# One more probability buffer, fewer copied scores, a regrouped load order and a five-block last unit in a fused attention and feed-forward kernel

## Chip, cores and metric

The kernel runs on one core of one Trainium2 chip. The metric is device time in microseconds for one execution. Before the change the median of three runs is 1485.19 us (1485.15 to 1485.42).

## What is computed

With x of 2048 tokens by 512 features, 32 heads of 16 and a hidden width of 1792:

```python
xn = layernorm(x)
q, k, v = split(xn @ wqkv)                       # 32 heads of 16
s = softmax(q @ k.T * 16 ** -0.5) @ v            # per head, all 2048 keys
s = concat_heads(s) @ wo
g = silu(ffn), ffn = (silu(xn @ w_gate) * (xn @ w_up)) @ w_down
out = x + s * g
```

All is float32. Most products are split in a high and a low part and take three matrix products.

## The kernel before, in words

**Three stages.** A prologue (0 to about 160 us) normalises x, projects q, k and v for four blocks of 512 tokens and writes them to DRAM (q_d, k_d, v_d, with row shifts for the exponentials in sh_d). Then comes the attention, with the feed-forward layer and the output projection woven into it as filler. A tail projects the last 512 tokens. The prologue's tile pools are closed before the attention's pools open, so the attention's tiles lie where prologue tiles lay, and their first writers wait for the last users of these, the store of v_d (L812 issues it) among them.

**Units and blocks.** A unit is one group of 4 heads (g) with one block of 512 queries (b): 8 x 4 = 32 units. A unit runs over 16 key tiles of 128 keys, cut into blocks of 4 to 6 key tiles (L448 to L462; units 27, 29, 30 and 31 have four blocks of 4, unit 28 has 6, 6, 4, the others 5s and one 6). There are 100 blocks, numbered from 0.

**Inside a block** (`run`, L837). For n key tiles there are 2n pairs (key tile, j), each with the scores of two heads. TensorE makes the two score products of a pair side by side on two halves of the array (L853). A pair goes one of two ways:
- *direct* ("D"): both products go to one of two double PSUM buffers (score0, score1); ScalarE takes the exponential of 128 x 1024 values straight into a probability buffer (L869), which frees the PSUM buffer.
- *copied* ("A", then "B"): the first head's product goes to a spare PSUM bank (acc1), VectorE copies it to a probability buffer (L881), then the second head's product goes to the same bank and is copied (L887). ScalarE takes the exponential in place later, after all direct ones of the block (L893).

Between them stands filler ("F"): pairs of half-array products (L188) of the feed-forward layer or of the output projection, in chunks that end in VectorE work on the banks bankx and banky. Feed-forward chunks have 24 products (gate and up, ended by the tanh of L219 on ScalarE and L220, L221 on VectorE) or 21 (down, ended by L238 and L239 or L242 and L243); chunks of the output projection have 9 or 12 (ended by L351 and L352). A block takes the length of the next chunk as its amount of filler. When all scores of a block are out, `values` (L373) multiplies the probabilities of its key tiles with v, four heads side by side into acc0 (L377). The program order on TensorE is thus: scores and filler of a block, its values, the next block.

**Who sets the order.** `events(n, f)` (L464) places D, A, B and F on a line of product slots by hand; the number of copied pairs comes from n and f. A block is written below as (n, f, copied), for example (6, 21, 3). VectorE's other work (splits of weights into high and low parts, normalising a finished unit) is a list of chores with costs, put between copies where the plan has room (L889), and the rest at the block's end. Each engine takes its instructions in program order. SP issues nearly all loads in program order, too: keys (`load_k`, six issues), values (`load_v`, one), queries (`load_q`, six), shifts (`load_shift`, two), gate and up weights (`load_gu`, two, L127) and down weights (`load_wd`, one, L150, into a single buffer). Keys and values have a ring of five chunks (kst, vst), queries two (qst).

**Buffers.** The probability buffers ("pr", 4 KB a partition each) are a ring of PROBS = 11, taken pair by pair in program order and freed when the values have read them. A block of 6 key tiles takes 12.

**Tail.** After the last block the rest of the filler runs (L916), then the last unit is normalised in two halves (L951 to L956: transpose, reciprocal, product, transpose), projected with wo (L932), gated and stored.

Of the kernel before, what the change touches and what calls it, by code (L numbers as in the profile page):

```python
# [9 lines left out]
F32 = mybir.dt.float32  # L10
# [9 lines left out]
P = 128  # L20
# [3 lines left out]
DH = 16  # L24
F = 1792
NB = 4
TB = S // NB
# [12 lines left out]
DC = D // HALF  # L40
LIMIT = 160.0
EARLY = 2
PROBS = 11
EPS = 1e-5
FINE = (27, 29, 30, 31)
QSLOT = (0, 1, 0)
# [4 lines left out]
def tile_block(ctx: ExitStack, tc: tile.TileContext, x, wqkv, wo, w_gate, w_up, w_down, out):  # L51
# [16 lines left out]
    two = ctx.enter_context(tc.tile_pool(name="two", bufs=2))  # L68
    pone = ctx.enter_context(tc.tile_pool(name="pone", bufs=1, space=PSUM))

    ident = const.tile([P, P], F32, name="ident")
    make_identity(nc, ident)
    bankx = pone.tile([P, 512], F32, name="bankx")
    banky = pone.tile([P, 512], F32, name="banky")
    banks = (bankx, banky)
# [40 lines left out]
    def load_v(g, c):  # L116
        sp.dma_start(vst[(g * NB + c) % RING], v_d[g][:, c * CT:(c + 1) * CT])
# [262 lines left out]
    def normalise(u, first, last, between=None):  # L380
        g, b = divmod(u, NB)
        n = last - first
        o1 = late.tile([P, TB], F32, tag="o1", name="o1")
        rl = late.tile([P, TB // 32], F32, tag="rl", name="rl")[:, :n // 32]
        ov = o1[:, :n].rearrange("p (c d) -> p c d", d=32)
        dst = on[b][:, first:last].rearrange("p (c s d) -> p c s d", s=2, d=DH)[:, :, g % 2]
        yield 3, partial(dve.transpose, o1[:, :n], acc[0][:, first:last])
        yield 1, partial(dve.reciprocal, rl, ov[:, :, DH])
        if between:
            yield 3, between  # L390
        yield 2, partial(dve.tensor_mul, dst, ov[:, :, :DH], rl[:, :, None].to_broadcast([P, n // 32, DH]))

    def finish(u):
        g, b = divmod(u, NB)
        chores.extend(normalise(u, 0, TB))
        if g % 2:
            o2 = late.tile([P, TB], F32, tag="o2", name="o2")

            def turn_out():
                dve.transpose(o2, on[b])  # L400
                if g < NG - 1 or b == NB - 1:
                    pool.dma_start(o_d[g // 2, b], o2)

            chores.append((3, turn_out))
            if g == NG - 1 and b < NB - 1:
                whole = (hh, wd, hh)[b].rearrange("p f j t -> p (f j) t")
                lhs[b, DT - 1] = whole[:, 2 * (DT - 1)], whole[:, 2 * DT - 1]

                def rounded():
                    dve.tensor_copy(lhs[b, DT - 1][0], o2)  # L410
                    ready[b] += 1

                chores.append((2, rounded))
                chores.append((3, lambda: dve.tensor_sub(lhs[b, DT - 1][1], o2, lhs[b, DT - 1][0].bitcast(F32))))

    settled = mybir.DependencyInfo(mybir.DependencyClass.Sync, mybir.DependencyReason.DATA)
    units = NG * NB
# [30 lines left out]
    blocks, opened = [], []  # L448
    for u in range(units):
        opened.append(len(blocks))  # L450
        if u in FINE:
            ns = [4] * 4
        elif u == units - 4:
            ns = [6, 6, 4]
        else:
            ns = [5] * 3
            far = sizes[len(blocks):len(blocks) + 3]
            ns[far.index(max(far)) if far[1] < max(far) else 1] = 6
        kt = 0
        for n in ns:  # L460
            blocks.append((u, kt, n))
            kt += n  # L462

    def events(n, f):  # L464
        length = 2 * n + f
        copied = max(0, 2 * n - max(2, (10 * length + 46) // 40)) if f else 0
        direct = 2 * n - copied
        gap = max(4, min(5, (length - 8) / max(1, direct - 2)))
        marks = [(0, "D"), (1, "D")] + [(7 + gap * i, "D") for i in range(direct - 2)]
        marks += [(4 + (length - 6) * i / (2 * copied), "AB"[i % 2]) for i in range(2 * copied)]  # L470
        marks.sort()
        out = []
        at = left = 0
        for t, kind in marks:
            while left < f - 1 and at < t:
                out.append((at, "F"))
                left += 1
                at += 1
            out.append((at, kind))
            at += 1 if kind == "D" else 0.5  # L480
        return direct, out + [(at + i, "F") for i in range(f - left)]

    with ExitStack() as pro:
# [4 lines left out]
        plast = pro.enter_context(tc.tile_pool(name="plast", bufs=1))  # L488
        pps = pro.enter_context(tc.tile_pool(name="pps", bufs=4, space=PSUM))

        xin = facc

        def load_tile(t):
# [85 lines left out]
        def turn(t):  # L579
            for c in range(DT):  # L580
                nc.tensor.transpose(acc[t % 2][:, c * P:(c + 1) * P], xn[t][:, c * P:(c + 1) * P], ident)  # L581
            return acc[t % 2].rearrange("p (c f) -> p c f", f=P)
# [239 lines left out]
    spare_bank = acc[1]  # L822
    ring(2, RING, att)
    queries(1, att)
    for c in range(2, NB):
        load_k(0, c)
        load_v(0, c)
    gate = [w.rearrange("p f j t -> p (f j) t")[:, 12 + i].bitcast(F32) for w in (hh, wd) for i in range(2)]
    on = [att.tile([P, TB], F32, name=f"on{b}") for b in range(NB)]

# [6 lines left out]
    def run(u, first, n):  # L837
        nonlocal lower
        g, b = divmod(u, NB)
        q = qst[u % 2]  # L840
        f = 0 if blocked() or not sizes else sizes.pop(0)
        direct, todo = events(n, f)
        if now == 0:
            for _ in range(4):
                todo.insert(0, todo.pop(max(i for i, (_, e) in enumerate(todo) if e == "F")))
        pairs = [(kt, j) for kt in range(first, first + n) for j in range(2)]
        straight, copies = pairs[:direct], pairs[direct:]
        probs, waiting = {}, []

        def scores(bank, kt, j, h):  # L850
            k, kc = kst[(g * NB + kt // CT) % RING], kt % CT
            r = slice(h * HALF, h * HALF + NROW)
            mm(bank, k[r, j, kc * P:(kc + 1) * P], q[r, j], start=True, stop=True)  # L853

        done = 0
        copying = [t + 1.5 for t, e in todo if e in "AB"]
        final = len(todo) - 1
        free = 0
        for at, (t, e) in enumerate(todo):
            if at == final:  # L860
                tidy()
            if e == "F":
                fill(1)
            elif e == "D":
                kt, j = straight[done]
                for h in order():
                    scores(score[done % 2][:, h], kt, j, h)
                probs[kt, j] = ppool.tile([P, 2, TB], F32, tag="pr", name="pr")
                act(probs[kt, j], score[done % 2], AF.Exp, scale=0.25)  # L869
                done += 1  # L870
                if done == 2:
                    while ends:
                        ends.pop(0)()
                    out_steps()
            elif e == "A":
                kt, j = copies.pop(0)
                waiting.append((kt, j))
                scores(spare_bank, kt, j, 0)
                lower = True
                probs[kt, j] = ppool.tile([P, 2, TB], F32, tag="pr", name="pr")  # L880
                dve.tensor_copy(probs[kt, j][:, 0], spare_bank)  # L881
                free = copying.pop(0) + 3
            else:
                kt, j = waiting[-1]
                scores(spare_bank, kt, j, 1)
                lower = False
                dve.tensor_copy(probs[kt, j][:, 1], spare_bank)  # L887
                free = copying.pop(0) + 3
            while chores and at < final and (not copying or max(free, t) + chores[0][0] <= copying[0] + 0.5):  # L889
                free = max(free, t) + chores[0][0]  # L890
                chores.pop(0)[1]()
        for kt, j in waiting:
            act(probs[kt, j], probs[kt, j], AF.Exp, scale=0.25)  # L893
        tidy()
        out_splits()
        catch_up()
        values(u, range(first, first + n), probs)

    for now, (u, first, n) in enumerate(blocks):
        g, b = divmod(u, NB)  # L900
        if first == 0 and u + 1 < units:
            load_q(u + 1)
            load_shift(u + 1)
        if first == 0 and g + 1 < NG and b == 0:
            load_k(g + 1, 0)
            load_v(g + 1, 0)
        run(u, first, n)
        if b == NB - 1 and g + 1 < NG:
            for c in range(NB - 1):
                if first < (c + 1) * CT <= first + n:  # L910
                    load_k(g + 1, c + 1)
                    load_v(g + 1, c + 1)
        if first + n == KT and u + 1 < units:
            ends.append(partial(finish, u))
# [80 lines left out]
```

## Time and profile before

| | |
|---|---|
| median of three runs | 1485.19 us |
| the profiled execution | 1483.91 us |
| its span, first to last instruction | 1482.1 us |
| mean granted TensorE clock | 0.989 |
| TensorE busy | 1448.6 us |
| ScalarE busy | 1091.7 us |
| VectorE busy | 765.3 us |
| GpSimd busy | 89.8 us |

The profile counts an engine busy while an instruction's record lasts. TensorE overlaps matmuls, so its share says little about waits between them. Rows in time give start, length, engine, line of the kernel, tiles written and read, and in brackets the idle time ahead with what ended it. PE is TensorE, PEld its weight loads, ACT ScalarE, DVE VectorE, POOL GpSimd, SPq the queue of loads. PEclk is the clock that TensorE was granted, as a share of the full one.

### The profile page before, as it was taken

To read this page: it belongs to the slowest core of one execution; us is meant where nothing else is said; L and a number is where in the kernel's file an instruction comes from. 1 tells how busy PE (TensorE), PEld (TensorE's weight loads), DVE (VectorE), ACT (ScalarE), POOL (GpSimd) and SP (SyncE) were. 2 spreads that over 40 slices of the span, in tenths; PEclk is the share of its full clock that TensorE was granted. 3 is DMA by queue.
4 is the path that set the end of the run, shared out by engine and by line. 5 is a ranking of instruction groups with operands and counts; after the bars stand their busy time and mean duration, and the time that the engine had idled before them with its cause. 6 is when DMAs were issued, how large, how long until landed. Compare 5 with 4: busy or idle time off the path is not lost.

```text
span 1482.1 us, 27795 instructions
## 1 busy us (share of the span) xinstructions
PE 1448.6 (98%) x11227; PEld 873.7 (59%) x11227; DVE 765.3 (52%) x1295; ACT 1091.7 (74%) x1235; POOL 89.8 (6%) x104
## 2 busy tenths in 40 slices
PE   9999799999999999999999999999999999999998
PEld 7777565566555665655566556665555665544444
DVE  5543255355545554555456435555554464455646
ACT  6733467787788888777887778888778787766674
POOL 4100200000000000000000000000000000001232
PEclk9999999999999999999999999999999999999999
DMA  6778632034544511345324202482342221323231
GB/s 222 262 242 255 145 76 55 12 84 94 115 101 104 127 33 34 71 117 124 92 74 117 53 18 70 105 172 62 83 102 58 55 69 55 90 72 118 83 114 66
DMA packets 126956, 148.17 MB, mean 100 GB/s; under 512 B 12524, under 2 KB 79340, under 8 KB 126052
## 3 DMA queue, kind: packets, MB, share of 16 engines
q1 hardware_dynamic: 121620, 125.79, 33.7%
q0 software_dynamic: 4912, 20.12, 3.7%
q8 instruction: 91, 1.49, 0.4%
q14 instruction: 45, 0.37, 0.1%
q10 hardware_dynamic: 288, 0.39, 0.1%
HBM read 106.68 MB, written 39.58 MB: 99 GB/s over the span
## 4 chain that ended last, share of the span: by engine, by line
PE 93%; DVE 3%; ACT 1%; DMA 1%; SPq 1%; issue 0%; DVEq 0%; ACTq 0%
PE acc L377 30%; PE bankx L188 23%; PE score L853 15%; PE banky L188 10%; PE ps L606 6%; PE acc L853 5%; PE ps L608 3%; DVE pr L881 1%; DMA wdr<-in_B_w_down_dram 1%; SPq L100 1%; DVE pr L887 1%; ACT pr L869 0%; PE acc L581 0%; ACT pr L893 0%; DMA v_d<-vt 0%
## 5 line engine op out<-in xcount | busy, mean ns | idle before, releaser
L869 ACT ACTIVATE pr<-score 128x1024 f32<-128x1024 f32 x854 | 813.6, 1028 | 293.2 <-PE score L853 258.9
L377 PE MATMUL acc<-pr,vst 128*17 128x512 f32 x4096 | 478.8, 596 | 0.0
L853 PE MATMUL score<-qst,kst 50*128 50x512 f32 x1708 | 420.5, 419 | 0.1
L188 PE MATMUL bankx<-fx,guh 64*128 64x512 f32 x896 | 313.4, 396 | 6.5 <-DVE ga L220 6.4
L188 PE MATMUL banky<-fx,guh 64*128 64x512 f32 x896 | 312.8, 396 | 0.4 <-DVE ga L221 0.3
L377 PEld LDWEIGHTS acc<-pr,vst 128*17 128x17 f32 x4096 | 114.6, 97 | 309.6 <-issue 269.4
L853 PEld LDWEIGHTS score<-qst,kst 50*128 50x128 f32 x1708 | 187.7, 186 | 137.1 <-issue 74.0
L881 DVE COPY pr<-acc 128x512 f32<-128x512 f32 x170 | 117.5, 691 | 189.4 <-PE acc L853 188.7
L188 PE MATMUL bankx<-wd,hh 64*128 64x512 f32 x672 | 205.6, 394 | 0.0
L188 PE MATMUL banky<-wd,hh 64*128 64x512 f32 x672 | 195.8, 394 | 0.0
L188 PEld LDWEIGHTS bankx<-fx,guh 64*128 64x128 f32 x896 | 167.9, 188 | 22.9 <-DVE ga L220 7.0
L188 PE MATMUL bankx<-fx,gul 64*128 64x512 f32 x448 | 177.4, 396 | 0.0
L188 PE MATMUL banky<-fx,gul 64*128 64x512 f32 x448 | 176.7, 394 | 0.0
L887 DVE COPY pr<-acc 128x512 f32<-128x512 f32 x170 | 117.6, 692 | 109.7 <-PE acc L853 99.6
L893 ACT ACTIVATE pr<-pr 128x1024 f32<-128x1024 f32 x170 | 172.8, 1064 | 0.0
L188 PEld LDWEIGHTS banky<-fx,guh 64*128 64x128 f32 x896 | 167.6, 188 | 5.9 <-DVE ga L221 1.9
L853 PE MATMUL acc<-qst,kst 50*128 50x512 f32 x340 | 144.8, 426 | 17.9 <-DVE pr L881 12.8
L188 PEld LDWEIGHTS bankx<-wd,hh 64*128 64x128 f32 x672 | 124.8, 187 | 13.8
L188 PEld LDWEIGHTS banky<-wd,hh 64*128 64x128 f32 x672 | 124.5, 186 | 5.0
L220 DVE SCALAR_TENSOR_TENSOR ga<-th,bankx 128x512 f32<-128x512 f32 x56 | 38.5, 687 | 154.7 <-ACT th L219 154.7
L853 PEld LDWEIGHTS acc<-qst,kst 50*128 50x128 f32 x340 | 63.7, 187 | 54.7 <-DVE pr L881 26.9
L188 PEld LDWEIGHTS bankx<-fx,gul 64*128 64x128 f32 x448 | 84.6, 189 | 6.7
(174 smaller groups left out, 1341.0 us busy)
## 6 DMA issues: line engine op xcount, KB each, us to landing
gur<-in_B_w_gate_dram SPq DMA_DIRECT2D x56, 256.0 KB
gur<-in_B_w_up_dram SPq DMA_DIRECT2D x56, 256.0 KB
wdr<-in_B_w_down_dram SPq DMA_DIRECT2D x56, 256.0 KB
kst<-k_d SPq DMA_DIRECT2D x192, 64.0 KB
qst<-q_d SPq DMA_DIRECT2D x192, 64.0 KB
fx<-xt_d SPq DMA_DIRECT2D x24, 512.0 KB
q_d<-parts SPq DMA_DIRECT2D x16, 512.0 KB
k_d<-parts SPq DMA_DIRECT2D x16, 512.0 KB
```

The lines of the kernel that those rows point to most:

```text
L100: sp.dma_start(dst[r:r + DH].bitcast(F32), src[part].rearrange("(j h d) t -> h d j t", j=2, h=2)[h])
L188: mm(banks[i], lhs[halves[i]], rhs[halves[i]], start=start, stop=stop)
L220: dve.scalar_tensor_tensor(ga, th, 1.0, bankx, op0=ALU.add, op1=ALU.mult)
L377: mm(acc[0][h * 32:h * 32 + DH + 1], v[:, kt % CT, h * (DH + 1):(h + 1) * (DH + 1)], probs[kt, h // 2][:, h % 2], start=kt == 0, stop=kt = ...
L606: mm(ps, w, a[:, c], start=n == 0, stop=n == 3 * DT - 1)
L608: mm(ps, a[:, c, tokens], w, start=n == 0, stop=n == 3 * DT - 1)
L853: mm(bank, k[r, j, kc * P:(kc + 1) * P], q[r, j], start=True, stop=True)
L869: act(probs[kt, j], score[done % 2], AF.Exp, scale=0.25)
L881: dve.tensor_copy(probs[kt, j][:, 0], spare_bank)
L887: dve.tensor_copy(probs[kt, j][:, 1], spare_bank)
L893: act(probs[kt, j], probs[kt, j], AF.Exp, scale=0.25)
```

## The change

- PROBS goes from 11 to 12. The room comes from two places: the identity matrix moves into a pool of the prologue, and the two 2 KB transpose buffers of `normalise` and `finish` ("o1", "o2") become one ("o"), taken when the work runs.
- `events` caps the copied pairs at (2 length - 5) // 22, where length is the number of scores and filler products, starts the copied products at slot 3 and puts them at least 5.6 slots apart. Block 0 gets no copied pair. Of the plan's blocks, (6, 21, 3) becomes (6, 21, 2), (4, 12, 2) and (4, 9, 3) become (4, 12, 1) and (4, 9, 1), and block 0 goes from one copied pair to none; (6, 24, 2), (5, 24, 1) and (5, 21, 2) keep their counts. In all, 148 pairs are copied, which were 170.
- The last unit is cut 4, 3, 3, 3, 3, so there are 101 blocks, as many as chunks of filler.
- Loads ahead of unit 0: the keys and values of chunk 3 are issued after block 0, the queries and shifts of unit 1 after block 1, the first keys and values of group 1 ahead of block 2. They all stood ahead of block 0's loads.

```diff
-PROBS = 11
+PROBS = 12
...
-    ident = const.tile([P, P], F32, name="ident")
-    make_identity(nc, ident)
...
     def normalise(u, first, last, between=None):
         g, b = divmod(u, NB)
         n = last - first
-        o1 = late.tile([P, TB], F32, tag="o1", name="o1")
-        rl = late.tile([P, TB // 32], F32, tag="rl", name="rl")[:, :n // 32]
-        ov = o1[:, :n].rearrange("p (c d) -> p c d", d=32)
+        turned = {}
...
+        def turn():
+            turned[0] = late.tile([P, TB], F32, tag="o", name="o")[:, :n]
+            dve.transpose(turned[0], acc[0][:, first:last])
...
     def finish(u):
...
-            o2 = late.tile([P, TB], F32, tag="o2", name="o2")
+            o = {}
 
             def turn_out():
-                dve.transpose(o2, on[b])
+                o[0] = late.tile([P, TB], F32, tag="o", name="o")
+                dve.transpose(o[0], on[b])
...
-        if u in FINE:
+        if u == units - 1:
+            ns = [4, 3, 3, 3, 3]
+        elif u in FINE:
             ns = [4] * 4
...
     def events(n, f):
         length = 2 * n + f
-        copied = max(0, 2 * n - max(2, (10 * length + 46) // 40)) if f else 0
+        need = 2 * n - max(2, (10 * length + 46) // 40)
+        copied = max(0, min(need, (2 * length - 5) // 22)) if now else 0
         direct = 2 * n - copied
         gap = max(4, min(5, (length - 8) / max(1, direct - 2)))
         marks = [(0, "D"), (1, "D")] + [(7 + gap * i, "D") for i in range(direct - 2)]
-        marks += [(4 + (length - 6) * i / (2 * copied), "AB"[i % 2]) for i in range(2 * copied)]
+        marks += [(3 + max(5.6, (length - 5) / (2 * copied)) * i, "AB"[i % 2]) for i in range(2 * copied)]
...
+        ident = pc.tile([P, P], F32, name="ident")
+        make_identity(nc, ident)
...
-    for c in range(2, NB):
-        load_k(0, c)
-        load_v(0, c)
+    load_k(0, 2)
+    load_v(0, 2)
...
     for now, (u, first, n) in enumerate(blocks):
         g, b = divmod(u, NB)
-        if first == 0 and u + 1 < units:
+        if first == 0 and 0 < u < units - 1:
             load_q(u + 1)
             load_shift(u + 1)
-        if first == 0 and g + 1 < NG and b == 0:
+        if now == 2 or first == 0 and 0 < g < NG - 1 and b == 0:
             load_k(g + 1, 0)
             load_v(g + 1, 0)
         run(u, first, n)
+        if now == 0:
+            load_k(0, NB - 1)
+            load_v(0, NB - 1)
+        elif now == 1:
+            load_q(1)
+            load_shift(1)
```

More of the change, by code (lines that the diff above doesn't have):

```diff
@@ L382, in normalise, with invert, scaled @@
         n = last - first
-        o1 = late.tile([P, TB], F32, tag="o1", name="o1")
-        rl = late.tile([P, TB // 32], F32, tag="rl", name="rl")[:, :n // 32]
-        ov = o1[:, :n].rearrange("p (c d) -> p c d", d=32)
+        turned = {}
         dst = on[b][:, first:last].rearrange("p (c s d) -> p c s d", s=2, d=DH)[:, :, g % 2]
-        yield 3, partial(dve.transpose, o1[:, :n], acc[0][:, first:last])
-        yield 1, partial(dve.reciprocal, rl, ov[:, :, DH])
+        def turn():
+            turned[0] = late.tile([P, TB], F32, tag="o", name="o")[:, :n]
+            dve.transpose(turned[0], acc[0][:, first:last])
+        def invert():
+            ov = turned[0].rearrange("p (c d) -> p c d", d=32)
+            turned[1] = late.tile([P, TB // 32], F32, tag="rl", name="rl")[:, :n // 32]
+            dve.reciprocal(turned[1], ov[:, :, DH])
+        def scaled():
+            ov = turned[0].rearrange("p (c d) -> p c d", d=32)
+            dve.tensor_mul(dst, ov[:, :, :DH], turned[1][:, :, None].to_broadcast([P, n // 32, DH]))
+        yield 3, turn
+        yield 1, invert
         if between:
             yield 3, between
-        yield 2, partial(dve.tensor_mul, dst, ov[:, :, :DH], rl[:, :, None].to_broadcast([P, n // 32, DH]))
+        yield 2, scaled
     def finish(u):
@@ L396, in finish @@
         if g % 2:
-            o2 = late.tile([P, TB], F32, tag="o2", name="o2")
+            o = {}
             def turn_out():
-                dve.transpose(o2, on[b])
+                o[0] = late.tile([P, TB], F32, tag="o", name="o")
+                dve.transpose(o[0], on[b])
                 if g < NG - 1 or b == NB - 1:
-                    pool.dma_start(o_d[g // 2, b], o2)
+                    pool.dma_start(o_d[g // 2, b], o[0])
             chores.append((3, turn_out))
@@ L409, in rounded @@
                 def rounded():
-                    dve.tensor_copy(lhs[b, DT - 1][0], o2)
+                    dve.tensor_copy(lhs[b, DT - 1][0], o[0])
                     ready[b] += 1
                 chores.append((2, rounded))
-                chores.append((3, lambda: dve.tensor_sub(lhs[b, DT - 1][1], o2, lhs[b, DT - 1][0].bitcast(F32))))
+                chores.append((3, lambda: dve.tensor_sub(lhs[b, DT - 1][1], o[0], lhs[b, DT - 1][0].bitcast(F32))))
     settled = mybir.DependencyInfo(mybir.DependencyClass.Sync, mybir.DependencyReason.DATA)
```

## The prediction, on record before the changed kernel ran

> **What bounds the kernel now.** I read the page first, then the stages (busy time by stretch), then the rows in time of one block of each form.
>
> ```profile
> span 1482.1 us, 27795 instructions
> PE 1448.6 (98%) x11227; PEld 873.7 (59%) x11227; DVE 765.3 (52%) x1295; ACT 1091.7 (74%) x1235; POOL 89.8 (6%) x104
> ```
>
> PE is counted busy almost throughout, but a matmul's record (0.39 us) is longer than its turn, so PE's share hides short waits. I therefore cut the span where the value products (L377) of a block end. Columns: stretch, length, busy PE, PEld, DVE, ACT, POOL (instructions), granted clock, DMA share, GB/s.
>
> ```profile
> 160.20:204.87 44.67, 32.47 (x230) 21.28 (x230) 18.16 (x29) 22.60 (x25) 6.44 (x6) 0.85 0.51 125
> 269.15:284.54 15.39, 15.39 (x116) 7.86 (x116) 5.54 (x8) 11.86 (x12) 0.00 (x0) 1.00 0.00 1
> 296.48:308.42 11.94, 11.94 (x104) 7.05 (x104) 6.05 (x10) 9.47 (x10) 0.00 (x0) 1.00 0.13 34
> 308.42:322.88 14.46, 14.46 (x122) 8.52 (x122) 7.73 (x13) 11.90 (x13) 0.00 (x0) 1.00 0.46 113
> 1284.93:1316.98 32.05, 30.63 (x230) 15.82 (x230) 16.84 (x28) 24.80 (x26) 0.78 (x2) 1.00 0.23 71
> 1316.98:1346.97 29.99, 25.28 (x134) 10.36 (x134) 20.76 (x37) 15.70 (x16) 0.54 (x1) 0.77 0.35 119
> 1346.97:1423.09 76.12, 72.04 (x506) 34.52 (x506) 38.61 (x57) 54.23 (x56) 21.78 (x20) 0.98 0.26 79
> 1423.09:1465.41 42.32, 40.44 (x290) 19.28 (x290) 24.05 (x34) 30.92 (x32) 13.26 (x13) 1.00 0.30 99
> 1465.41:1482.10 16.69, 10.85 (x54) 7.38 (x54) 9.92 (x20) 0.81 (x2) 4.58 (x4) 0.94 0.26 96
> ```
>
> In order: the first two blocks; a block of 6 key tiles with 21 filler products and 3 copied pairs, "(6,21,3)"; a (5,21,2); a (6,24,2); blocks 85 and 86, both (6,21,3); 87 and 88, both (4,9,3); 89 to 95, all (4,12,2); the last unit, four (4,12,2); the tail. The (5,21,2) is at TensorE's own pace: 31 products (10 of scores, 21 filler), then five key tiles of values at 4.49 us (row 176.74 below), leave 7.45/31 = 0.24 us a product. The others carry waits.
>
> **The twelfth buffer and the 6-tile blocks.** Rows of the (6,24,2): ACT three times, PE twice, PEld.
>
> ```profile
> 308.94 8.49 ACT L869 ACTIVATE pr<-score 128x1024 f32<-128x1024 f32 x9 [2.44 <-PE score L853]
> 318.38 1.02 ACT L869 ACTIVATE pr<-score 128x1024 f32<-128x1024 f32 x1 [0.95 <-PE acc L377]
> 319.78 2.01 ACT L893 ACTIVATE pr<-pr 128x1024 f32<-128x1024 f32 x2
> 316.57 0.50 PE L853 MATMUL score<-qst,kst 50*128 50x512 f32 x2
> 317.24 5.64 PE L377 MATMUL acc<-pr,vst 128*17 128x512 f32 x48
> 321.84 0.12 PEld L377 LDWEIGHTS acc<-pr,vst 128*17 128x17 f32 x4 [0.19 <-ACT pr L893]
> ACT pr L869 <- PE acc L377: 25.7, 26, 1.2
> ```
>
> Two things show. Nine exponentials start back to back, (8.49 - 1.03)/8 = 0.93 us apart, and the tenth score product (316.57) begins as the eighth ends (308.94 + 7 x 0.93 + 1.03 = 316.5): two score buffers make ACT the pace, and the values start 0.74 us after that end. **So the scoring of a block with d direct pairs lasts at least 0.52 + 0.93 (d-3) + 1.03 + 0.74 us** (0.52 from the end of the block before, at 308.42, to the first exponential); d = 10 gives 8.8, as here. Second, the tenth exponential waits 0.95 us for value products (the last row: 26 such waits between 204.9 and 1229, one per 6-tile block): 12 pairs, 11 buffers. That pushes the copied exponentials back, and the last key tile waits. Five tiles take 4.49 us, so six take 5.36; here 5.64. With 12 buffers the 0.28 goes: 21 blocks x 0.28 = **5.9 us**.
>
> (6,21,3):
>
> ```profile
> 270.61 0.69 DVE L881 COPY pr<-acc 128x512 f32<-128x512 f32 x1 [4.39 <-PE acc L853]
> 277.15 0.69 DVE L887 COPY pr<-acc 128x512 f32<-128x512 f32 x1 [0.59 <-PE acc L853]
> 279.59 1.02 ACT L869 ACTIVATE pr<-score 128x1024 f32<-128x1024 f32 x1 [1.11 <-PE acc L377]
> ```
>
> These are the first and last of six copies, (277.15 - 270.61)/5 = 1.31 us apart where the plan has 4.5 products (1.08 us): one spare bank makes a chain of product and copy, and it holds TensorE. After, it is two pairs 7 products apart and ten direct: by the formula 8.8, plus 5.36 of values, 14.2 against 15.3 (five blocks, 15.19 to 15.39): **5.6 us**. Blocks 85 and 86 also start behind VectorE's splits: 14.4 each, 32.05 - 28.8 = **3.2**.
>
> **The short blocks.** One (4,12,2): its first and last copy, its first exponentials, its values.
>
> ```profile
> 1359.14 0.69 DVE L881 COPY pr<-acc 128x512 f32<-128x512 f32 x1 [4.23 <-PE acc L853]
> 1363.05 0.69 DVE L887 COPY pr<-acc 128x512 f32<-128x512 f32 x1 [0.59 <-PE acc L853]
> 1358.21 2.88 ACT L869 ACTIVATE pr<-score 128x1024 f32<-128x1024 f32 x3 [1.63 <-PE score L853]
> 1364.11 4.15 PE L377 MATMUL acc<-pr,vst 128*17 128x512 f32 x32
> ```
>
> Four copies 1.30 apart; scoring takes 1364.11 - 1357.67 = 6.44, values 4.15, 10.6 in all. After: one copied pair, seven direct. By the formula scoring 0.52 + 3.73 + 1.03 + 0.74 = 6.0 (TensorE alone: 20 x 0.24 = 4.8); values unheld 4.49 x 4/5 = 3.6, since the seventh and the copied exponential end at 8.2 and the fourth tile starts at 8.6. Sum 9.65. Blocks 89 to 95: 76.12 - 7 x 9.65 - 0.6 (block 94, where VectorE's splits still come first) = **8.0**. Blocks 87 and 88 lose more to the same chain (three pairs, granted clock 0.77); after, also seven direct, with 0.1 for splits ahead of the copy: 29.99 - 19.5 = **10.5**.
>
> Last unit: one such block, then four of three tiles (five direct, one copied): scoring 18 products, 4.4; values 2.75, 0.15 of them spent waiting for the copied exponential, 7.3. 9.65 + 29.3 + 0.4 for gate chores = 39.3 against 42.32: **3.0**. The fifth block takes the 12 filler products that now run after the last values.
>
> Tail:
>
> ```profile
> 1468.49 0.69 DVE L351 TENSOR_SCALAR y<-bankx 128x512 f32<-128x512 f32 x1 [3.49 <-PE banky L188]
> 1469.89 0.44 DVE L953 STREAM_TRANSPOSE o<-acc 128x256 f32<-128x256 f32 x1
> 1472.59 0.72 PE L932 MATMUL score<-fx,rh 128*128 128x512 f32 x2 [1.22 <-ACT rh L956]
> ```
>
> The last transpose stands behind L351 on VectorE, which waits for that filler. After, it starts at the end of the values; TensorE first has 12 products (2.8 us), then the 9.5 us from 1472.59 to the end, 0.2 of it saved: 12.1 against 16.69, **4.6**.
>
> **The opening.**
>
> ```profile
> 166.29 1.24 DVE L144 CAST hh<-ga 128x512 fp32r<-128x512 f32 x1 [8.31 <-DMA v_d<-vt]
> 171.62 0.76 PE L853 MATMUL acc<-qst,kst 50*128 50x512 f32 x1 [5.80 <-DVE pr L881]
> 169.43 2.76 SPq L100 DMA_DIRECT2D kst<-k_d  x6
> 176.74 4.49 PE L377 MATMUL acc<-pr,vst 128*17 128x512 f32 x40
> 180.21 0.67 SPq L127 DMA_DIRECT2D gur<-in_B_w_gate_dram  x1
> 181.67 0.56 SPq L150 DMA_DIRECT2D wdr<-in_B_w_down_dram  x1
> 186.48 0.43 DVE L891 CAST wd<-wdr 128x512 fp32r<-128x512 f32 x1 [13.38 <-DMA wdr<-in_B_w_down_dram]
> 188.29 0.79 PE L188 MATMUL bankx<-fx,guh 64*128 64x512 f32 x1 [6.40 <-DVE ga L220]
> ```
>
> VectorE, in order, stands at L144 until the v_d store has landed, so block 0's copy is late and the pair's second product holds TensorE 5.8 us. Without copies the block goes on at ACT's pace (8.8 us, and 0.6 for the tanh ahead of its last three), and its values end near 175.5, not 181.2. Then L220 decides: it frees bankx for the next filler, behind the split of w_down on VectorE. That load was issued at 181.67, behind 22 others (kst3, vst3, qst1, its shift, kst4, vst4) that SP issued from 169.43 to 180.21. All 22 go behind the first blocks' weight loads: the issue comes 10.8 us earlier, at 170.9, lands 4.8 later (as now), and 1.8 later again filler starts, at 177.5 against 188.3. The rest of block 1 took 16.6 us, partly at half clock; after, 14.2 - 0.6 + 1.0 (the first copy stands behind five VectorE operations). **10.8 + 2.0 = 12.8 us.** The moved loads have cover: kst3 is issued near 174 and read from about 192; qst1, now also behind the second w_down load, which waits for VectorE at 176.6, is out by 181 and read near 204; kst4 is for unit 4. Without that cover each such load costs what w_down's did, 4.8 us. Bounds for the whole: if w_down lands 3 us later among the kst3 loads, 9.5; if TensorE never waits for L220, 14.5.
>
> **At nothing.** The identity's new place: same instructions, ahead of the same work. One transpose buffer "o" for two: a transpose now waits for the o_d store before it, which has a unit (36 us or more) to land; uncovered, 12 stores at no more than w_down's 4.8 us each, as many bytes. The shifted marks in (5,24,1) and (5,21,2): same counts, 0.25 products earlier to 0.75; they run without a wait, bounds -1 and +2 us over 53 blocks.
>
> **Sum.** 12.8 + 5.9 + 5.6 + 3.2 + 8.0 + 10.5 + 3.0 + 4.6 = 53.6. The profiled execution took 1483.91 (span 1482.1 and 1.8 around it): 1430.3. The median of before is 1.28 above it: **1431.6 us**.
>
> **Rivals.** *Half clock (slower).* The short blocks leave TensorE about 1 us idle near the end of scoring, where it waits for ACT.
>
> ```profile
> 1319.80:1323.20 3.40, 2.19 (x11) 1.08 (x11) 1.63 (x4) 1.02 (x1) 0.00 (x0) 1.00 0.00 0
> 1323.20:1330.10 6.90, 6.29 (x28) 2.32 (x30) 4.77 (x9) 4.06 (x5) 0.00 (x0) 0.51 0.21 49
> ```
>
> A stretch with TensorE busy 64% was followed by two at half clock. If each block from 87 to 100 fell under that, its 8.4 us of TensorE work would double against 9.65: about +7 each for 14 blocks, 98 us, so 1530; it turns the sign from 8 blocks on. Against it: with about 0.7 us of visible gap in 3.4 a stretch stays 79% busy, and blocks 89 to 100 now run with gaps at full clock but for one. Chance 0.03. [...]
>
> *VectorE, not the copy chain, holds the short blocks*: its splits and gate work sit ahead of the one copy left, and 87 to 100 gain a third of what I count: 14 less, 1446. For it: DVE is busy 20.76 of 29.99 us in 87 and 88. Against: in 89 to 99 it is busy half the time, and copies go away. 0.13.
>
> *The opening's load is late anyway*: SP is free earlier, but kst and weight loads share the DMA engines (share 0.51 in that stretch) and w_down lands 6 us later; 7 less, 1438.5. Against: the same loads stood ahead of it before. 0.12.
>
> *The twelfth buffer doesn't do it*: D10's exponential finds another wait (the score banks) and the last tile waits as now: 5.9 and some 2 of the (6,21,3) are not had, 1439.5. Against: the row names value products as what ended the wait. 0.10.
>
> **Numbers.** Mine 0.62: 1431.6, its own range 1424 to 1438. Range 1422 to 1447: the lower end takes the good bounds (opening 14.5, short blocks 3 better, half-clock losses gone), the upper one the three milder rivals singly; two together, or half clock, lie outside. A measurement tells about 0.2% from no change: faster 0.96, same 0.01, slower 0.03.
>
> **What would show it.** Right: no wait of ACT L869 for value products; 6-tile blocks at 14.2 with either filler; 4-tile blocks with 12 filler at 9.6; values of block 0 ending near 175.5 and filler again by 178; end within 12.5 us of the last values; 148 pairs copied, not 170. Wrong: a granted clock under 0.9 from block 87 on, a copy waiting over 1.5 us behind VectorE's splits, a qst1 or kst3 load that scores wait for.

## The result, and the profile after

The changed kernel takes **1436.18 us** (median of four runs, 1435.62 to 1437.09) against 1485.17 (four runs, 1483.27 to 1485.42): 0.9673 of before, 95% interval 0.9657 to 0.969. The profiled execution took 1435.62 us, with a mean granted clock of 0.996. The page:

```profile
span 1433.8 us, 27758 instructions
...
PE 1409.6 (98%) x11227; PEld 860.7 (60%) x11227; DVE 734.7 (51%) x1251; ACT 1080.5 (75%) x1235; POOL 89.9 (6%) x104
...
L896 DVE COPY pr<-acc 128x512 f32<-128x512 f32 x148 | 102.2, 690 | 176.7 <-PE acc L868 173.7
```

The count of matmuls is the same, 11227, and the span is 48.3 us shorter; 148 pairs are copied (L896 is the first copy of a pair). The stages, cut as before at the end of each block's values, in the same columns as the prediction's table (stretch, length, busy time of PE, PEld, DVE, ACT, POOL, granted clock, DMA share, GB/s):

```profile
160.20:195.70 35.50, 31.15 (x230) 18.18 (x230) 17.20 (x27) 22.30 (x25) 6.45 (x6) 0.90 0.63 157
259.72:273.87 14.15, 13.73 (x116) 7.60 (x116) 4.15 (x6) 11.27 (x12) 0.00 (x0) 1.00 0.00 1
285.80:297.74 11.94, 11.94 (x104) 7.08 (x104) 6.05 (x10) 9.43 (x10) 0.00 (x0) 1.00 0.11 34
297.74:311.90 14.16, 14.16 (x123) 8.23 (x122) 8.04 (x13) 11.78 (x13) 0.00 (x0) 1.00 0.45 111
1264.00:1292.89 28.89, 27.76 (x230) 15.75 (x230) 15.36 (x27) 23.67 (x26) 1.32 (x3) 1.00 0.24 79
1292.89:1314.10 21.21, 18.94 (x134) 8.22 (x134) 15.48 (x28) 15.02 (x16) 0.00 (x0) 0.92 0.50 169
1314.10:1382.73 68.63, 63.48 (x506) 31.90 (x506) 27.35 (x40) 52.47 (x56) 21.07 (x20) 1.00 0.27 87
1382.73:1421.73 39.00, 38.44 (x313) 21.16 (x313) 21.38 (x30) 30.07 (x32) 15.84 (x14) 1.00 0.33 116
1421.73:1433.80 12.07, 7.46 (x31) 5.18 (x30) 8.53 (x18) 0.81 (x2) 2.75 (x3) 0.90 0.29 109
```

Row by row these answer to the nine rows of before. What each stage gave, beside what the prediction counted (us of span):

| Stage | before | after | gain | predicted |
|---|---|---|---|---|
| blocks 0 and 1 | 44.67 | 35.50 | 9.2 | 12.8 |
| 21 blocks (6,24,2) | 306.5 | 300.0 | 6.6 | 5.9 |
| five blocks (6,21) | 76.5 | 70.8 | 5.7 | 5.6 |
| blocks 85, 86 | 32.05 | 28.89 | 3.2 | 3.2 |
| blocks 87, 88 | 29.99 | 21.21 | 8.8 | 10.5 |
| blocks 89 to 95 | 76.12 | 68.63 | 7.5 | 8.0 |
| last unit | 42.32 | 39.00 | 3.3 | 3.0 |
| tail | 16.69 | 12.07 | 4.6 | 4.6 |
| 53 five-tile blocks | 653.4 | 653.9 | -0.5 | 0 |
| sum | | | 48.4 | 53.6 |

The prologue (160.20 us) and the four blocks of unit 27 (43.6 us), which the table leaves out, took the same time in both.

The opening is where most of the difference lies. Its rows in time, SP's queue first:

```profile
166.05 3.57 SPq L98 DMA_DIRECT2D kst<-k_d  x6
171.58 0.55 SPq L148 DMA_DIRECT2D wdr<-in_B_w_down_dram  x1
176.39 0.43 DVE L906 CAST wd<-wdr 128x512 fp32r<-128x512 f32 x1 [5.12 <-DMA wdr<-in_B_w_down_dram]
177.46 0.68 DVE L218 SCALAR_TENSOR_TENSOR ga<-th,bankx 128x512 f32<-128x512 f32 x1
178.20 0.50 PE L186 MATMUL bankx<-fx,guh 64*128 64x512 f32 x1 [2.82 <-DVE ga L218]
```

w_down is issued 10.1 us earlier than before (181.67), lands after the same 4.8 us, and filler starts at 178.20 instead of 188.29. Block 0's values end at 174.7 and block 1's first four score products at 175.4; TensorE then stands 2.8 us until the filler. Now the same execution cut on the edges at which the granted clock changes:

```profile
175.27:178.68 3.41, 0.59 (x3) 0.18 (x1) 2.15 (x4) 1.85 (x2) 0.00 (x0) 1.00 0.92 196
178.68:182.09 3.41, 3.12 (x14) 2.55 (x15) 3.34 (x7) 0.00 (x0) 0.00 (x0) 0.50 1.10 247
182.09:185.51 3.42, 3.42 (x18) 2.88 (x18) 1.13 (x2) 2.05 (x2) 0.00 (x0) 0.50 0.56 120
185.51:188.92 3.41, 3.41 (x32) 2.63 (x32) 1.47 (x3) 3.18 (x4) 0.00 (x0) 1.00 0.58 172
```

After the gap come two stretches with TensorE busy and at half clock: 14 and 18 matmuls where the next stretch has 32. By these counts about 3 us of work are lost (an estimate). The prediction had no half clock in block 1.

### The profile page after: what moved, and what is told of

It reads as the page before. It is cut to its first block, busy times and chain, and to the rows that moved or that the text cites. A ratio compares the mean times of both kernels' runs of the same rounds, so it can differ in the third digit from the quotient of the medians.

```text
span 1433.8 us, 27758 instructions
## 1 busy us (share of the span) xinstructions
PE 1409.6 (98%) x11227; PEld 860.7 (60%) x11227; DVE 734.7 (51%) x1251; ACT 1080.5 (75%) x1235; POOL 89.9 (6%) x104
## 4 chain that ended last, share of the span: by engine, by line
PE 91%; ACT 4%; DVE 2%; DMA 1%; issue 1%; SPq 0%; DVEq 0%; ACTq 0%
PE acc L375 30%; PE bankx L186 23%; PE score L868 15%; PE banky L186 9%; PE ps L622 6%; ACT pr L884 4%; PE ps L624 3%; PE acc L868 3%; DMA wdr<-in_B_w_down_dram 1%; PE acc L597 0%; DMA v_d<-vt 0%; DMA wraw<-in_A_wqkv_dram 0%; DVE hh L276 0%; PE ps L653 0%; SPq L98 0%
## 5 line engine op out<-in xcount | busy, mean ns | idle before, releaser
L884 ACT ACTIVATE pr<-score 128x1024 f32<-128x1024 f32 x876 | 823.9, 1030 | 260.5 <-PE score L868 260.0
L375 PE MATMUL acc<-pr,vst 128*17 128x512 f32 x4096 | 460.9, 595 | 0.0
L868 PE MATMUL score<-qst,kst 50*128 50x512 f32 x1752 | 412.1, 420 | 10.8 <-ACT pr L884 10.5
L186 PE MATMUL bankx<-fx,guh 64*128 64x512 f32 x896 | 320.2, 394 | 3.3 <-DVE ga L218 3.2
L868 PEld LDWEIGHTS score<-qst,kst 50*128 50x128 f32 x1752 | 177.3, 184 | 169.9 <-issue 74.8
L186 PE MATMUL bankx<-wd,hh 64*128 64x512 f32 x672 | 199.2, 392 | 0.0
L896 DVE COPY pr<-acc 128x512 f32<-128x512 f32 x148 | 102.2, 690 | 176.7 <-PE acc L868 173.7
L902 DVE COPY pr<-acc 128x512 f32<-128x512 f32 x148 | 102.2, 691 | 102.5 <-PE acc L868 92.1
L908 ACT ACTIVATE pr<-pr 128x1024 f32<-128x1024 f32 x148 | 153.5, 1083 | 0.0
L868 PE MATMUL acc<-qst,kst 50*128 50x512 f32 x296 | 118.1, 399 | 1.6 <-DVE pr L896 1.5
L218 DVE SCALAR_TENSOR_TENSOR ga<-th,bankx 128x512 f32<-128x512 f32 x56 | 38.5, 687 | 137.9 <-ACT th L217 137.9
L186 PEld LDWEIGHTS banky<-fx,gul 64*128 64x128 f32 x448 | 84.1, 188 | 1.6
```

What stands on the lines that cost most here:

```text
L186: mm(banks[i], lhs[halves[i]], rhs[halves[i]], start=start, stop=stop)
L218: dve.scalar_tensor_tensor(ga, th, 1.0, bankx, op0=ALU.add, op1=ALU.mult)
L375: mm(acc[0][h * 32:h * 32 + DH + 1], v[:, kt % CT, h * (DH + 1):(h + 1) * (DH + 1)], probs[kt, h // 2][:, h % 2], start=kt == 0, stop=kt = ...
```

## The experiments

Eight kernels, each a small edit of the changed one ("after", 1436.18). They ran in two groups, each beside the kernel before: the first four beside 1485.73 us (seven runs), the others beside 1484.85 (seven runs); after itself ran beside 1485.17. Between groups, then, a difference of 1 us says little. The theory in all of them is the prediction's: in-order queues in the opening, the chain of product and copy in the short blocks, the twelfth buffer in the 6-tile ones. Stages are read from the one profiled execution of each, totals from the medians.

### One: eleven buffers again

```diff
-PROBS = 12
+PROBS = 11
```

> The changed kernel with 11 probability buffers again. My theory: the twelfth pair of each 6-tile block waits again for value products (about 28 waits of 1 us on ScalarE), and the values of a 6-tile block take 5.6 us and not 5.34; 29 such blocks by 0.28 us give +8 us, about 1444. Rival, the twelfth buffer is not what matters (the wait on the score buffers ends as late anyway): within 2 us of the changed kernel, 1436.

Measured: **1441.62 us** (1441.35 to 1441.8), 0.9703 of before (0.9687 to 0.9719), 5.4 over after. The wait is back (view of waits: engine, tile and line that wait, what ended it; us, times, us of the longest):

```profile
ACT pr L884 <- PE acc L375: 27.6, 29, 1.0
```

The (6,24,2) blocks go back to a median of 14.46 and their values to 5.64: +6.8 in all. The (6,21,2) blocks wait as well but keep 14.16, so the expectation, which counted all 29 blocks of 6 key tiles, was too high. The 27.6 us of waits are worth 6.8, and, but for 0.3 us in block 86, only in the blocks with 24 filler products. There the last key tile's weight load waits again for a copied exponential, as it did before the change:

```profile
312.27 0.12 PEld L375 LDWEIGHTS acc<-pr,vst 128*17 128x17 f32 x4 [0.19 <-ACT pr L908]
```

After's ScalarE in a (6,24,2):

```profile
298.27 9.41 ACT L884 ACTIVATE pr<-score 128x1024 f32<-128x1024 f32 x10 [2.49 <-PE score L868]
307.54 0.63 ACT L217 ACTIVATE th<-bankx 128x512 f32<-128x512 f32 x1
308.01 2.03 ACT L908 ACTIVATE pr<-pr 128x1024 f32<-128x1024 f32 x2
```

Ten exponentials in one row, where before had nine, a wait and one. The tanh, which only the chunk of 24 has, comes between them and the two copied ones; with it the row is long enough for the last key tile to be late. Other stages came out differently too: the opening is 0.8 longer, but block 88 takes 10.0 instead of 11.6, without half clock (granted clock 1.00 from 1300.92 to 1311.15), and so the total rose by less than the 6.8.

### Two: the old count and places of copied pairs, except in block 0

```diff
-        copied = max(0, min(need, (2 * length - 5) // 22)) if now else 0
+        copied = max(0, need) if now else 0
...
-        marks += [(3 + max(5.6, (length - 5) / (2 * copied)) * i, "AB"[i % 2]) for i in range(2 * copied)]
+        marks += [(4 + (length - 6) * i / (2 * copied), "AB"[i % 2]) for i in range(2 * copied)]
```

> The changed kernel with the old number and places of copied pairs, except in block 0, which stays without. My theory, the chain of product and copy on one spare bank: the five blocks of 6 tiles with 21 filler go back to some 14.8 (12 buffers stay), 85 and 86 to 15.5 each, 87 and 88 to about 15 each, the eight blocks of 4 tiles with 12 filler to 10.6 each: 3 + 2 + 9 + 8.5 = +22 us, about 1458. Rival, VectorE's splits hold the short blocks and not the chain: blocks 89 to 96 change by less than 0.3 us each, +10 at most, 1446.

Measured: **1456.17 us** (1454.0 to 1457.6), 0.9804 (0.9786 to 0.9821), 20.0 over after. Blocks 87 and 88 take 15.95 and 14.56, 89 to 95 take 75.11, the last unit 40.00. One block of 4 key tiles:

```profile
1335.61:1346.19 10.58, 10.13 (x74) 4.80 (x74) 4.15 (x6) 7.73 (x8) 3.20 (x4) 1.00 0.45 150
```

10.58, as before the change, with VectorE busy 4.15 of it: not VectorE's load but the chain sets the length. Part of the 20.0 is the clock: over blocks 87 and 88 (1305.25 to 1335.76) the granted clock was 0.83 here, against 0.92 in after. That is as much as three stretches of 3.41 us at half clock against one, each of them worth up to 1.7, half its length (an estimate). Where the count of copied pairs is the same in both plans, the old places change nothing: the 21 (6,24,2) blocks take 300.0 us in both kernels, the 53 five-tile blocks 653.4 against 653.9. The (6,21,3) blocks take 14.55 here, against 15.31 before and 14.16 after: the twelfth buffer alone gives 0.76 of the 1.15 a block, the new plan alone (experiment one) all of it. The two gains overlap; they don't add up.

### Three: the last unit in four blocks

```diff
-            ns = [4, 3, 3, 3, 3]
+            ns = [4] * 4
```

> The changed kernel with the last unit in four blocks of 4 tiles. My theory: four blocks at 9.6 are 38.4 us (now 39.0 in five), but the last 12 filler products run after the last values again, and the tail takes 16.5 and not 12.1: +4, about 1440. Rival, the tail is bounded by the stores at its end whatever comes ahead: within 1 us, 1436.

Measured: **1441.2 us** (1440.21 to 1441.88), 0.9698 (0.9682 to 0.9714). Unit and tail together take 38.67 + 16.65 against 39.00 + 12.07 after: +4.25 of the +5.0. The tail, and the VectorE operation that waits for the leftover filler:

```profile
1423.15:1439.80 16.65, 10.83 (x54) 7.35 (x54) 10.22 (x21) 0.81 (x2) 5.31 (x4) 1.00 0.26 96
```

```profile
1426.23 0.69 DVE L349 TENSOR_SCALAR y<-bankx 128x512 f32<-128x512 f32 x1 [2.77 <-PE banky L186]
```

The fifth block costs 0.3 and takes 4.6 off the end.

### Four: the 22 loads ahead of block 0 again

```diff
-    load_k(0, 2)
-    load_v(0, 2)
+    for c in range(2, NB):
+        load_k(0, c)
+        load_v(0, c)
+    load_q(1)
+    load_shift(1)
+    load_k(1, 0)
+    load_v(1, 0)
```

(The three later places are dropped.)

> The changed kernel with the 22 opening loads back ahead of block 0 and still no copied pair in block 0. My theory: block 0 ends its values near 174.7 as now, but w_down is issued near 181 and filler starts at 188; TensorE idles 13 us and block 1 ends at 204.9 as before the change: +9 us, 1445, all of what the opening gained. Rival, the copied pair was worth half of it: block 1 ends near 200, +4.5, 1441.

Measured: **1444.22 us** (1443.38 to 1447.63), 0.9718 (0.9702 to 0.9735), 8.0 over after. Opening, from the profiled execution (the longest of the four):

```profile
160.20:206.45 46.25, 30.72 (x232) 17.71 (x230) 17.19 (x27) 22.24 (x25) 6.44 (x6) 0.82 0.52 120
```

```profile
183.62 0.55 SPq L148 DMA_DIRECT2D wdr<-in_B_w_down_dram  x1
188.22 0.43 DVE L911 CAST wd<-wdr 128x512 fp32r<-128x512 f32 x1 [16.15 <-DMA wdr<-in_B_w_down_dram]
```

Block 0 ends at 175.22 as after, but w_down is issued at 183.62 and block 1 ends at 206.45, later even than before (204.87). In this execution the two blocks gain nothing without the load order; by the medians the kernel loses 8.0 us, where the two blocks had gained 9.2.

### Five: a copied pair in block 0 again

```diff
-        copied = max(0, min(need, (2 * length - 5) // 22)) if now else 0
+        copied = max(0, min(need, (2 * length - 5) // 22))
```

> The changed kernel with one copied pair in block 0 again, the loads in their new order. My theory, the two opening waits lie side by side: TensorE is held until 171.6 again and block 0 ends near 181, but by then w_down has been split (177), so nothing more is waited for and the clock is full again; block 1 ends within 1 us of 195.7 and the time is that of the changed kernel, 1436. Rival, the two waits add up: block 1 ends near 201, +5.8, 1442.

Measured: **1434.72 us** (1433.75 to 1435.39), 0.9656 (0.9635 to 0.9676), 1.5 *under* after, little more than the groups' times of before differ by. Block 0 now ends at 180.41, behind the copy that waits for VectorE, but the w_down split at 177.20 passes meanwhile, and block 1 follows without a gap:

```profile
180.41:194.57 14.16, 14.16 (x122) 7.95 (x122) 9.21 (x15) 11.83 (x13) 0.00 (x0) 1.00 0.65 156
```

14.16 at full clock, ending 1.1 earlier than after. So leaving the copy out of block 0 brought nothing: its wait lay beside the wait for w_down. The shorter block 0 only moved TensorE's idle time to where half clock followed in a busy block (2.82 us up to 178.20, half clock from 178.68 to 185.51). Here the granted clock was 0.90 over the two blocks and 1.00 in block 1, so the half clock, some 6.9 us (an estimate: 0.10 of 34.37 us, twice), lay in block 0, which has the wait.

### Six: no wait for w_down ahead of the first filler

The split of the second w_down tile is moved behind block 1's copies, and its load goes into the idle "o" buffer, so that VectorE doesn't stand behind this load when L218's counterpart is due.

```diff
-        raw = one.tile([P, D], F32, tag="wdr", name="wdr")
+        raw = late.tile([P, D], F32, tag="o", name="wdr") if i == 1 else one.tile([P, D], F32, tag="wdr", name="wdr")
...
-                        if n == 3 * DC - 2 and now >= 0:
+                        if n == 3 * DC - 2 and now >= 0 and i != 1:
+                            if i == 2:
+                                split_wd(1, 1)
                             split_wd(f, i)
```

> The changed kernel with the split of the second w_down tile moved behind block 1's copies (its load goes to the idle transpose buffer, so the next load need not wait for it). L220 then stands behind nothing that waits for a load. My theory: TensorE doesn't idle after block 0, its clock stays full, and block 1 ends near 189 instead of 195.7: -6.8 us, 1429.4. Rival, another load (gate and up weights, kst2) is as late: block 1 ends at 193 or later, -2.5 at most, 1434.

Measured: **1430.03 us** (1429.8 to 1430.3), 0.9626 (0.9606 to 0.9645), 6.2 under after.

```profile
160.20:188.93 28.73, 27.42 (x230) 15.88 (x230) 17.28 (x27) 22.14 (x25) 6.45 (x6) 1.00 0.70 164
```

```profile
171.41 0.68 DVE L220 SCALAR_TENSOR_TENSOR ga<-th,bankx 128x512 f32<-128x512 f32 x1
```

The operation that frees bankx runs 6.1 us earlier (177.46 after), the gap is gone, the granted clock is 1.00 over the two blocks (0.90 in after), and they end 6.8 earlier: 2.8 of that is the gap, and most of the rest the clock (an estimate: half of 6.83 us is 3.4).

### Seven: no copied pair in the blocks with 12 or fewer filler products

```diff
-        copied = max(0, min(need, (2 * length - 5) // 22)) if now else 0
+        copied = max(0, min(need, (2 * length - 5) // 22)) if now and f > 12 else 0
```

> The changed kernel with no copied pair in blocks with 9 or 12 filler products (14 blocks). My theory, direct pairs are paced by two score buffers: 4 tiles with eight direct pairs score in 0.52 + 5 x 0.93 + 1.03 + 0.74 = 6.95 us, 10.6 with values (now 9.6), and 3 tiles with six direct in 5.1, 7.9 (now 7.3): 10 x 1.0 + 4 x 0.6 = +12 us, 1448. Rival, fewer copies are always better, since TensorE then waits for no copy: 9.3 for 4 tiles, -3 us, 1433.

Measured: **1448.68 us** (1445.54 to 1449.98), 0.9744 (0.972 to 0.9768), 12.5 over after. A block of 4 key tiles here, and the same block's ScalarE:

```profile
1329.56:1340.04 10.48, 9.28 (x74) 4.31 (x74) 1.39 (x2) 7.44 (x8) 3.22 (x4) 1.00 0.45 150
```

```profile
1330.09 7.44 ACT L884 ACTIVATE pr<-score 128x1024 f32<-128x1024 f32 x8 [3.03 <-PE score L868]
```

and after's, with one copied pair (the block runs from 1323.70 to 1333.30, its values from 1329.67):

```profile
1324.23 6.55 ACT L884 ACTIVATE pr<-score 128x1024 f32<-128x1024 f32 x7 [2.10 <-PE score L868]
1324.93 0.69 DVE L896 COPY pr<-acc 128x512 f32<-128x512 f32 x1 [3.27 <-PE acc L868]
1326.54 0.69 DVE L902 COPY pr<-acc 128x512 f32<-128x512 f32 x1 [0.92 <-PE acc L868]
```

Eight exponentials take 7.44 and hold the scoring, seven take 6.55: each direct pair costs (7.44 - 6.55) = 0.89. With none, one and two copied pairs the block takes 10.48, 9.60 and 10.58 (experiment two). One is the best: with none ScalarE is the pace, with two the copy chain. The 3-tile blocks say the same (7.79 with none, 7.28 with one). Two of the 4-tile blocks, 88 and 95, took 12.2 here, 1.7 more than 10.48: one stretch of 3.41 us at half clock in each would account for it (an estimate; the run's mean granted clock is 0.995). Fewer copies isn't better as such.

### Eight: six, and block 94's splits between its copies

Six splits of the output projection's left side stood ahead of block 94's first copy. They become chores with costs, which the plan puts between the copies.

```diff
+        if now == opened[units - 2] + 2:
+            for c in range(DT - 1):
+                chores.append((2, partial(dve.tensor_copy, lhs[2, c][0], parts_o[2, c])))
+                chores.append((3, partial(low_part, c)))
+
+    def low_part(c):
+        dve.tensor_sub(lhs[2, c][1], parts_o[2, c], lhs[2, c][0].bitcast(F32))
+        ready[2] += 1
...
-        if now == opened[units - 2] + 1:
-            split_out(2)
```

> The late split of w_down as in the kernel beside it, and also the six splits that stood ahead of block 94's first copy made chores of that block, put between its copies. My theory: block 94 goes from 11.1 to 9.7 us, so 1.4 less than the kernel beside it, 1428. Rival: the splits on VectorE are slowed by GpSimd's work wherever they stand, and hold something else up: within 0.5 us of the kernel beside it, 1429.4.

Measured: **1428.36 us** (1427.35 to 1429.42), 0.9612 (0.9591 to 0.9633): 7.8 under after and the shortest of all. Blocks 87 and 88, then block 94:

```profile
1289.74:1309.33 19.59, 17.34 (x134) 8.08 (x134) 14.38 (x26) 15.03 (x16) 0.00 (x0) 1.00 0.55 179
1357.29:1366.89 9.60, 9.01 (x75) 4.50 (x74) 5.30 (x9) 7.49 (x8) 3.25 (x4) 1.00 0.26 84
```

Block 94 takes 9.60 like its neighbours, where after has

```profile
1362.06:1373.14 11.08, 9.43 (x74) 4.70 (x74) 5.90 (x9) 7.60 (x8) 3.59 (x4) 1.00 0.21 72
```

with its first copy at 1365.27, 3.2 us into the block where its neighbour above has 1.2 (1324.93 - 1323.70). Against experiment six the whole is 1.7 less, and 1.5 is this block. In the two profiled executions the rest evens out: block 88 is 1.5 shorter here, without half clock, and block 1 ends 1.4 later.

## Why the prediction was right, and where it was off

The time is inside the range and 4.6 us above the forecast. The steps hold; the size of the opening was off.

- **The opening** is the mis-sized term: 9.2 for 12.8. *"the issue comes 10.8 us earlier, at 170.9, lands 4.8 later (as now)"*: it came at 171.58, because the six key loads ahead took SP 3.57 us instead of their 2.66 before, so filler started 0.7 late. The rest of block 1, *"after, 14.2 - 0.6 + 1.0"*, 14.6, took 17.5, from 178.20 to 195.70: 2.9 more. Experiment five shows block 1 at 14.16 and experiment six at 14.17 when no idle stretch stands ahead of its filler, both at a granted clock of 1.00, and two stretches of 3.41 us at half clock can cost 3.4 (an estimate: half of 6.83): the 2.9 is put down to the clock. Experiment two has a longer gap (3.7 us, filler from 178.89), and the rest of its block 1 takes 15.7, 1.5 over 14.16: about what one such stretch would cost (1.7, an estimate). I had worked out the gap (175.5 to 177.5) and treated it as lost time only, although in my own row of the half-clock rival a partly idle stretch (2.19 us busy of 3.40) was followed by half clock (0.51).
- **What made the opening faster** was the load order (experiment four), as said. That block 0 without copies ends near 175.5 held too (174.7), but it was worth nothing (experiment five).
- **The twelfth buffer**: 0.28 a block, as worked out, and the rival against it falls: no ScalarE wait for value products is left, and experiment one brings the 29 waits and the 0.28 back. Not said: it matters only where the tanh lengthens ScalarE's row. The (6,21,2) blocks don't need it.
- **The copy chain**: undoing the plan alone costs 20.0 us (experiment two, some of it half clock: 0.83 over blocks 87 and 88), and the formula gave 14.2, 9.65 and 7.3 for blocks that take 14.16, 9.60 and 7.28. It also gave 10.6 and 7.9 for the blocks without copies in experiment seven (10.48 and 7.79). The change's floor of 5.6 products between copies does nothing here: (length - 5)/(2 copied) is 6.0 to 14.5 in every form that has copies. So it is the cap on the count that works, and since a turn of the chain, 1.31 us, is about 5.5 products of 0.24, the cap is what keeps the plan above it.
- **VectorE holds the short blocks** (rival, 0.13) falls as a whole, and was right in two places: block 94, 11.08 for the 10.25 I allowed, and block 88, where the first copy runs 2.0 us into the block behind splits and a transpose, 0.8 later than its neighbour's:

```profile
1304.45 0.63 DVE L896 COPY pr<-acc 128x512 f32<-128x512 f32 x1
```

- **Blocks 87 and 88**: 8.8 for 10.5. The late copy costs block 88 0.4 (10.0 against 9.6 where it runs at full clock), a stretch at half clock (1308.49 to 1311.90) another 1.6. The clock is in the gain as well: before the change the two blocks held four such stretches (granted clock 0.77), after it one (0.92). **Half clock**, the rival that I gave 0.03 to, didn't turn the sign, but it is in the result twice, for some 4.5 us (2.9 in block 1, 1.6 in block 88: 11.6 where it ran at 10.0 in experiments one, three and eight). That is the larger part of the forecast's error. In the changed kernel no short block after 88 had it (granted clock 1.00 from 1314.10 to 1421.73).
- **The load is late anyway** (rival, 0.12) falls: issue to use is 4.8 us, as before (171.58 to 176.39).
- **Tail and last unit** as worked out (4.6 and 3.3); experiment three puts the tail's gain on the fifth block. After the last values (they end at 1421.73) VectorE, idle until then, turns to the transpose:

```profile
1421.81 0.45 DVE L386 STREAM_TRANSPOSE o<-acc 128x256 f32<-128x256 f32 x1 [1.32 <-PE acc L375]
```

- **At nothing**: the 53 five-tile blocks lost 0.5, within the bounds.

The clock in block 88, by stretches on the edges at which the grant changes, and block 94's partly idle stretch:

```profile
1305.08:1308.49 3.41, 2.22 (x13) 1.35 (x15) 2.75 (x5) 3.10 (x4) 0.00 (x0) 1.00 1.01 335
1308.49:1311.90 3.41, 3.41 (x20) 0.66 (x20) 2.56 (x5) 2.41 (x3) 0.00 (x0) 0.50 1.04 387
1311.90:1315.32 3.42, 3.42 (x32) 1.40 (x26) 1.91 (x4) 0.68 (x1) 0.00 (x0) 1.00 0.13 48
1363.11:1366.52 3.41, 2.21 (x19) 1.64 (x17) 2.77 (x5) 2.35 (x3) 0.75 (x2) 1.00 0.28 106
```

From the edge at 178.68 in the opening to the one at 1308.49 here are 1129.81 us, 331 times 3.4133, and in the execution of before from 169.53 to 1323.24 are 1153.71, 338 times 3.4133. In these two executions every change of the granted clock that the trace shows (5 in after, 11 before) lies on one grid of 3.413 us. The grid does not lie at the same place in both: 178.68 is 1.19 us past a multiple of 3.4133, 169.53 is 2.28. So the same idle time can fall into one stretch or be shared by two. The same code of block 88 ran without half clock in experiment one:

```profile
1304.33:1307.74 3.41, 2.37 (x18) 0.85 (x22) 1.00 (x2) 3.41 (x5) 0.00 (x0) 1.00 0.05 17
1307.74:1311.15 3.41, 3.41 (x34) 1.35 (x28) 3.31 (x7) 1.28 (x2) 0.00 (x0) 1.00 0.43 111
```

In the executions of before and after, every full-clock stretch of this grid with TensorE busy 36% or less was followed by half clock (0.59 of 3.41 us from 175.27 and 1.23 from 1427.96 in after; 0.64 of 3.42 from 1476.83 and two with none, from 166.12 and 183.18, before), and none busy over 71% was. Between these both occur: 65% in both of after's rows above, one with and one without; before, 64% twice, with half clock behind it from 1401.74 (2.18 of 3.41) and without from 1470.01 (2.19). In experiment six a stretch busy 70% had half clock behind it (2.39 of 3.42, from 1298.90). What decides in that band is open: the records of matmuls are longer than their turns (0.39 us against 0.24), so the share is rough. By these rows 1.2 us of idle time in a stretch of 3.41 can come ahead of half clock (2.22 busy, from 1305.08) or not (2.21, from 1363.11).

## What to carry to other kernels

When a hand-written order mixes two ways out of PSUM, work out the turn of each (here 0.93 us for a direct pair, 1.31 us for each copy through one spare bank) and give the slower chain no more than fits in the block; the best share can be one, with none and two both worse. Ahead of the first busy stretch, look at what stands in front of the one load that frees an engine: 22 loads in an in-order queue cost 8 us here, and one split that could wait cost another 6. A gap of TensorE cost more than its length here where half clock followed in busy work: 2.82 us of gap, then 6.83 us at a granted clock of 0.50 with about 3 us of work lost (an estimate from the counts of matmuls). So a wait was better moved to where little work followed (experiment five, 1.5 us under after, little more than the groups differ by) or taken out (experiment six, 6.2 under) than merely shortened.

## What the runs showed of the hardware that was not expected

- In the executions of before and after the granted clock changed only on a grid of 3.413 us (11 and 5 changes), whose place against the kernel differed between the two. In after, the opening's 2.82 us gap was followed by two such stretches (6.83 us) at a granted clock of 0.50, block 88's partly idle one (2.22 us busy of 3.41) by a single one. The first half-clock stretch was busy 91% in the one case (3.12 of 3.41) and 100% in the other; what brought the full clock back was not found.
- Two of VectorE's six split operations ahead of block 94's first copy took two to four times as long as the others (1.66 us for 0.69, 1.52 for 0.42). Both ran beside tensor operations of GpSimd. After's VectorE, and GpSimd at the same time (start, length):

```profile
1360.46 1.66 DVE L276 TENSOR_TENSOR hh<-hh 128x512 fp32r<-128x512 f32 x1
1362.04 1.52 DVE L275 CAST hh<-hh 128x512 fp32r<-128x512 f32 x1
1363.60 0.69 DVE L276 TENSOR_TENSOR hh<-hh 128x512 fp32r<-128x512 f32 x1
1364.20 0.42 DVE L275 CAST hh<-hh 128x512 fp32r<-128x512 f32 x1
```

```profile
1360.19 1.38 POOL L334 TENSOR_TENSOR y<-y,gt 128x512 f32<-128x512 f32 x1 [6.06 <-DVE y L350]
1361.65 1.63 POOL L335 TENSOR_TENSOR pair<-y,pair 128x512 f32<-128x512 f32 x1
```

  The cast that runs beside L335 takes 1.52 us, the next one, when L335 has ended, 0.42; the subtraction beside L334 takes 1.66, the next one 0.69. Before the change the same two rows stand beside the same work (1.66 at 1397.72, 1.50 at 1399.30). Beside other work of GpSimd it was not always so: in after's opening, with memsets of GpSimd from 166.10 to 172.82, the subtraction at 167.37 takes 0.69, though the cast at 166.09 takes 1.25.
- Six key loads kept SP's queue 3.57 us in the changed kernel (the first row of the opening above) and 2.66 before:

```profile
166.26 2.66 SPq L100 DMA_DIRECT2D kst<-k_d  x6
```

  Before, another group of six, issued at 176.15, took 3.55, so it is not the change alone. What lengthens them is open.
